# Transposes inside attention visits, a later last value product and sums behind the squares, in an attention and feed-forward kernel on one core

## The chip, the core and the metric

The kernel runs on one core of a Trainium2 chip. Five engines work beside each other, each through its own instructions in order: TensorE (PE in the profile, with its weight loads as PEld), VectorE (DVE), ScalarE (ACT), GpSimd (POOL) and SyncE (SP, which here only issues transfers). Transfers are issued from the queues of SP, POOL and ACT. The metric is the device time of one execution in microseconds (us), as the median of several.

## What is computed

Eight batches of 448 rows go through a squared-ReLU attention with 12 heads of 64, and the result through layer normalisation and a two-layer feed-forward block with a residual:

```python
scores = scale * np.matmul(q, k.transpose(0, 1, 3, 2))      # 8 x 12 x 448 x 448
attn = np.maximum(scores, 0.0) ** 2 / S
x = np.matmul(attn, v)                                      # heads side by side: 8 x 448 x 768
mu = np.mean(x, axis=-1, keepdims=True)
var = np.mean((x - mu) ** 2, axis=-1, keepdims=True)
xn = (x - mu) / np.sqrt(var + 1e-06) * g_ln
ch = np.maximum(xn @ w_ch1, 0.0) @ w_ch2                    # 768 -> 3072 -> 768
return x + ch
```

Inputs and output are float32; the products run in bfloat16.

## The kernel before

**Groups, batches, pairs.** The 12 heads of a batch are handled in three groups of four (`G` = 3), so there are 24 groups, numbered n = 3 b + m. Two batches make a pair; the feed-forward runs by pairs (four of them). A head's 448 rows are seven slices of 64 (`J` = 7).

**Attention of one group.** `scores` (L392) fills a PSUM tile with the products of one slice of keys (or two, in the first two batches) with the queries, on TensorE split into 64x64 tiles; ScalarE applies ReLU and moves it to SBUF (L411). The square is left to VectorE later: a tile waits in the list `later` (batches 0 and 1) or `fresh` (the others) until `squares_now` (L383) or `square_fresh` (L377) puts the multiplication into VectorE's order, at L389 or L380. Some squares run on ScalarE at once (L413). `values` (L421) multiplies by v (28 products, `av_ps`), and VectorE scales the result into `xT` (L438). Before a group's scores, queries and keys must be turned. For batches 0 and 1 TensorE does it: `piece` (L269) issues 14 transposes of 128x64 into one PSUM tile and a copy moves it out (L281); `transposes` (L286) calls it for q and for k. The later batches use transposing transfers from SP.

**PSUM.** Scores, value products and batch 1's transposes share three tiles (`ps_sc`); the feed-forward's results have two banks of their own (`ps_mm`). A tile that is asked for again waits until its last reader is done.

**Batch 1.** `attention_block(1, BLK[1][0])` makes a list of units for its first four slices: groups 3, 4 and 5, two score units each, one unit of transposes ahead of each group, a last value product and a centring. `interleave` (L13) sets them between the 26 units of batch 0's first feed-forward layer (`ffn1`, L718, six products into one `ps_mm` bank; `ffn1_head` takes three such at once). After the first ScalarE or VectorE work of a visit, `ffn1` lets VectorE move out the result of the one unit that follows a visit (`since`, L737), and ScalarE the next ones; right after it, it puts the waiting squares into VectorE's order.

**The three long stages.** For the pairs 0, 1 and 2 the second feed-forward layer of the pair runs beside the attention of the next two batches. `spread` (L28) takes the layer's parts (three products each) one by one and puts in a unit of attention when its share of work is due. A unit of attention is a bundle of three score slices, in some of them with the value product of the group before. After every other part `spread` puts one waiting square into VectorE's order, and before a bundle all of them. Between bundles come units of cost 0, the hooks: "even" after the first batch's values and "odd" when only the last group's values are missing. They make sums for the next layer-one stage, among them x[6] at L994, x[5] at L989 and, in the third stage, transfers on SP. When the units are used up or the parts end, the last value product comes, then "start" with the sums L905 and L906, then the parts that were held back (`few`), then the layer-one stage (`run`, L1017), which makes a 2x2 block product from seven products of half size. Its first steps combine partial results on VectorE at L1026, L1028, L1042 and L1045, and in the first pair weight sums at L936.

**What sets the order.** Each engine takes its instructions in the order in which the program issues them, so the Python order above is each queue's order.

Of the kernel before, what the change touches and what calls it, by code (L numbers as in the profile page):

```python
# [27 lines left out]
def spread(main, cost, side, costs, pending):  # L28

    period = (cost * len(main) + sum(costs)) / sum(c > 0 for c in costs)
    at, due, done, n, ago = 0, period - costs[0], 0, 0, 0
    for unit in main:
        unit()
        at += cost
        ago += 1
        if ago % 2:
            pending(1)
        if n < len(side) and at >= (due if costs[n] else done + 3 * cost):  # L40
            if costs[n]:
                pending()
            side[n]()
            if costs[n]:
                at += costs[n]
                due += period
                done = at
                ago = 0
            n += 1
    for unit in side[n:]:  # L50
        pending()
        unit()
    pending()
# [3 lines left out]
def kernel(  # L57
# [32 lines left out]
    J = S // HP  # L90
# [84 lines left out]
    def load(n, names):  # L175
        if n >= len(groups):
            return
        b, m = groups[n]
        for name in names:
            if b == 1 and name != "v":  # L180
                o = (2 * m + "qk".index(name)) * 2 * S
                t = hold[:, o:o + 2 * S].rearrange("p (r s) -> p r s", r=2)
            elif name == "q":
                t = qbuf[m][:, D:D + 2 * S].rearrange("p (r s) -> p r s", r=2)
            else:
                t = slot(name, n)
            nc.gpsimd.dma_start(t, srcs[name][b][:, m:NP:G, :])  # L187
            qkv[name, b, m] = t
# [72 lines left out]
    def idle(n):  # L261

        for _ in range(n):
            nc.tensor.matmul(idle_ps[:, 0, :P], ones, ones, start=True, stop=True)
# [4 lines left out]
    def piece(sb, b, m, n, lo, hi, bank=True):  # L269

        if b == 0 and bank:
            ps = ps_mm.tile([P, 1024], bf16, tag="mm", name="tr_ps")
        else:
            ps = ps_sc.tile([P, 2, 1024], bf16, tag="sc", name="tr_ps")[:, 0]
        src, i = qkv[n, b, m], "qk".index(n)
        for j in range(lo, hi):
            for pr in range(2):
                nc.tensor.transpose(  # L278
                    ps[pr * HP:(pr + 1) * HP, j * P:(j + 1) * P],
                    src[:, pr, j * D:(j + 1) * D], identity)  # L280
        return lambda copy, lo=lo, hi=hi: copy(  # L281
            sb[:, i * J + lo:i * J + hi, :], ps[:, lo * P:hi * P].rearrange("p (j c) -> p j c", c=P))

    held = []

    def transposes(b, m):  # L286


        if b == 0:
            o = 12 * 1024 + m * 2 * J * P  # L290
            sb = early[:, o:o + 2 * J * P].rearrange("p (i c) -> p i c", c=P)
        elif m:
            o = (m - 1) * 2 * J * P
            sb = hold[:, o:o + 2 * J * P].rearrange("p (i c) -> p i c", c=P)
        else:
            sb = slot("qT", G)
        dve, act = nc.vector.tensor_copy, nc.scalar.copy
        if (b, m) == (0, 0):
            nc.vector.tensor_copy(identity_g, identity[:K1, :K1])

            cast(dve, "q", 0, FEW)
            cast(act, "k", 0, FEW)
            cast(act, "k", FEW, J)
            idle(30)
            piece(sb, b, m, "q", 0, FEW)(dve)
            idle(2)
            piece(sb, b, m, "k", 0, FEW)(dve)
            idle(5)
        else:
            q_of = piece(sb, b, m, "q", 0, J)  # L310
            if (b, m) == (0, 1):

                q_of(act, 0, FEW)
            else:
                q_of(dve)
            k_of = piece(sb, b, m, "k", 0, J)
            if (b, m) == (0, 2):
                k_of(dve, 0, 3)
                held.append(lambda: k_of(act, 3, J))
            elif (b, m) == (0, 1):  # L320
                k_of(dve, 0, 3)
                k_of(dve, 3, J)
                q_of(dve, FEW, J)
            else:
                k_of(dve)
        if b:
            squares_now()
        st[b, m] = {
            "q": lambda i, r: sb[:, 0:J],
            "k": lambda i: sb[:, J + i],  # L330
            "where": lambda pr, j: (j, pr),
            "attn": [], "sb": sb}
# [209 lines left out]
    def transposed(n):  # L542

        if groups[n][0] < by_dma:
            transposes(*groups[n])
            return


        if by_dma * G < n < LATE:
            load(n + 2, "kq")  # L550
        keys_dma(n)
        queries_dma(n)
        if n == LATE + 1:
            put_off.append((n + 2, "kq"))
        elif n >= LATE:
            load(n + 2, "kq")

    def attention_block(b, blk):


        lo, hi, first = b * G, b * G + G, blk[0] == 0
        units = [lambda: transposed(lo)] if first else []

        def unit(n, part):
            squares_now()
            for i in range(4 * part, min(4 * part + 4, J), 2):
                scores(n, tuple(range(i, min(i + 2, J))), blk)
            if b == 1 and not first and part and n == hi - 1:
                transposed(hi)
            if part and n > lo:  # L570
                values(n - 1, blk)
                if not first:
                    load(n + 3, "v")
        for n in range(lo, hi):
            units.append(lambda n=n: unit(n, 0))
            if first and n + 1 < hi:
                units.append(lambda n=n: transposed(n + 1))
            units.append(lambda n=n: unit(n, 1))

        def last():  # L580
            values(hi - 1, blk)
            if b == 1 and not first:
                load(hi + 3, "v")
        units.append(last)
        units.append(lambda: centre(b, blk))
        return units
# [813 lines left out]
    for pair in range(pairs - 1):  # L1400
        last = pair == pairs - 2
        following = {}

        def hook(name):
            if not following:
                following.update(ffn1_pair(
                    pair + 1, keep=pair == 0, given=pair > 0, late=last,
                    between=(between_one, between_two, between_three)[pair]))
                if pair:
                    tokens_room(pair + 1)  # L1410
            following[name]()
            if (pair, name) in soon:
                tokens_part(pair + 1, *soon[pair, name])
        if last:
            mm = [ps_mm.tile([P, 512], fp32, tag="mm", name="o_ps") for _ in range(2)]
            zs = [x_room.rearrange("p b c s -> p (b c s)")[:, 3 * KH * P:3 * KH * P + 2 * DH].bitcast(fp32),
                  room0[:, 9:].rearrange("p c n -> p (c n)").bitcast(fp32)]
            h_sum_tiles()
            head, units, _ = strassen_units(pair, mm, lambda t: mm[::-1] if t % 2 else mm)
        else:  # L1420
            units = ffn2_units(pair)
            head, units = (units[:PARTS // 2], units[PARTS // 2:]) if pair else ([], units)
        if pair:
            for unit in head:
                unit()
            stage["close"]()
            if pair == 1:
                odd_h_out(pair, nc.sync, (8, KH), (8 + KH, K2))
            narrow.close()
            ps_sc = open_wide()  # L1430
        else:
            units = fold_beside(units)
        if pair == 1:
            w2_sum_tiles()
            units = beside_of(units, dict(zip((20, 36, 50), w2_sum_units("t6"))))
        beside, costs, left = attention(
            [2 * pair + 2, 2 * pair + 3], {G - 1: lambda: hook("even"), 2 * G - 2: lambda: hook("odd")})
        few = 3 * PARTS // 4
        spread(units[:-few], K2 // PARTS * DH, beside, costs, square_fresh)
        for f in left:  # L1440
            f()
        wide.close()
        hook("start")
        ps_m = open_narrow()
        for unit in units[-few:]:
            unit()
        store_now()
        stage = following
        if pair == 0:
            tokens(pair + 1)  # L1450
        stage["run"]()
        if pair == 0:
            statistics(pair + 1, 0)
            roots(pair + 1, 0, 1)
# [44 lines left out]
```

## Time and profile before

| | |
|---|---|
| median of 3 runs | 513.37 us (512.39 to 513.43) |
| time of the profiled execution | 512.57 us |
| its span in the trace | 510.6 us |
| PE busy | 503.1 us (99%), granted clock 1.0 |
| PEld / DVE / ACT / POOL busy | 297.9 / 388.2 / 315.3 / 130.0 us |
| stretch of batch 1's first part beside layer one | about 38 to 64 us |
| long stages (layer two beside attention) | 99 to 167, 214 to 274 and 321 to 390 us |
| layer-one stages between them | 167 to 214, 274 to 321 and 390 to 437 us |

The profile's page gives the busy time of each engine, the span in slices and the chain of work that ended last, followed back from the last instruction. The views of the trace used here are that chain in order of time (start, length, what) and the timeline (start, length, engine, line, operation, tiles; in brackets how long the engine had been idle and who ended it). TensorE's ends are modelled, so its starts and the chain's lengths are the better measure.

### The profile page before, as it was taken

The numbers are of one execution on the slowest core, as the hardware profiler recorded it, in microseconds if no ns is written. First come the engines' busy times: TensorE is split into PE (matmuls) and PEld (weight loads), VectorE is DVE, ScalarE is ACT, GpSimd is POOL, SyncE is SP. The second block draws the span as 40 slices with busy tenths as digits, with TensorE's granted clock in tenths as the row PEclk, the third lists the DMA queues.
The fourth block names the chain that finished last, engine by engine and source line by source line (L and its number), as shares of the span: only waits on it lengthen the run. The fifth ranks groups of instructions, "written<-read, shape, count | busy, mean of one in ns | idle before, by whom it ended". The sixth has DMA issues, their size and how long they took to land.

```text
span 510.6 us, 11501 instructions
## 1 busy us (share of the span) xinstructions
PE 503.1 (99%) x4545; PEld 297.9 (58%) x4545; DVE 388.2 (76%) x747; ACT 315.3 (62%) x519; POOL 130.0 (25%) x180
## 2 busy tenths in 40 slices
PE   8999999999999999999999999999999999999996
PEld 6677778955555555555555555555555555566663
DVE  4875755697998988768878888578869688677663
ACT  5966776578887566667883666489884677300000
POOL 8335102011412486002111995011000231000000
PEclk9999999999999999999999999999999999999999
DMA  9999999999999975739993878349936943622222
GB/s 198 206 206 206 211 206 143 135 195 177 203 203 223 219 228 152 191 87 163 269 170 75 177 167 140 61 78 179 194 69 164 224 131 94 230 64 63 63 62 62
DMA packets 136743, 80.25 MB, mean 157 GB/s; under 512 B 92418, under 2 KB 132610, under 8 KB 136690
## 3 DMA queue, kind: packets, MB, share of 16 engines
q1 hardware_dynamic: 106402, 46.59, 43.9%
q0 software_dynamic: 28272, 29.92, 36.7%
q10 hardware_dynamic: 2016, 3.02, 2.4%
q8 instruction: 35, 0.57, 0.5%
q14 instruction: 18, 0.15, 0.1%
HBM read 66.65 MB, written 19.86 MB: 169 GB/s over the span
## 4 chain that ended last, share of the span: by engine, by line
PE 92%; DMA 5%; POOL 1%; ACT 1%; DVE 1%; issue 1%; DVEq 0%; ACTq 0%; POOLq 0%
PE m_ps L960 28%; PE o_ps L789 17%; PE m_ps L1175 11%; PE o_ps L1175 11%; PE h_ps L728 7%; PE sc_ps L400 7%; PE av_ps L432 6%; DMA w<-in_moe_w_ch_dram 3%; PE h_ps L773 2%; DMA v_sb<-in_v_dram 2%; PE o_ps L1136 2%; PE h_ps L755 1%; ACT attn_sb L411 1%; PE tr_ps L278 1%; PE sum_ps L465 0%
## 5 line engine op out<-in xcount | busy, mean ns | idle before, releaser
L411 ACT ACTIVATE attn_sb<-sc_ps 128x896 bf16<-128x896 f32 (+4 forms) x150 | 126.2, 902 | 27.1 <-PE sc_ps L400 20.8
L964 ACT ACTIVATE hT_sb<-m_ps 128x448 bf16<-128x448 f32 x144 | 78.2, 543 | 51.8 <-PE m_ps L960 49.1
L789 PE MATMUL o_ps<-w,hT_sb 128*128 128x384 bf16 x528 | 92.2, 327 | 0.0
L789 PEld LDWEIGHTS <-hT_sb 128*128 128x128 bf16 x528 | 49.0, 98 | 39.8 <-issue 10.1
L380 DVE TENSOR_TENSOR attn_sb<-attn_sb 128x896 bf16<-128x896 bf16 x93 | 55.6, 617 | 8.0 <-ACT attn_sb L411 8.0
L728 PE MATMUL h_ps<-x_room,w 128*128 128x192 bf16 (+2 forms) x384 | 44.0, 263 | 0.2 <-DMA w<-in_moe_w_ch_dram 0.2
L438 DVE TENSOR_SCALAR xT_sb<-av_ps 128x896 bf16<-128x896 f32 (+2 forms) x30 | 27.1, 903 | 22.3 <-PE av_ps L432 22.2
L1175 PEld LDWEIGHTS <-hT_sb 128*128 128x128 bf16 x312 | 30.0, 98 | 21.6 <-issue 2.1
L1175 PEld LDWEIGHTS <-x_room 128*128 128x128 bf16 x288 | 27.5, 98 | 20.2 <-issue 2.5
L728 PEld LDWEIGHTS <-w 128*128 128x128 bf16 x384 | 33.8, 97 | 7.2 <-issue 1.8
L960 PEld LDWEIGHTS <-w 128*128 128x128 bf16 x246 | 24.0, 97 | 22.7
L1042 DVE TENSOR_TENSOR m_ps<-x_room,m_ps 128x448 f32<-128x448 f32 x36 | 22.6, 628 | 18.4 <-ACT hT_sb L964 18.2
L413 ACT ACTIVATE attn_sb<-attn_sb 128x896 bf16<-128x896 bf16 x33 | 31.4, 950 | 1.0
L960 PEld LDWEIGHTS <-w_sum 128*128 128x128 bf16 x210 | 20.5, 98 | 19.3 <-DVE w_sum L936 0.4
L705 DVE BATCH_NORM_STATS2 stats<-xtok_sb 128x6 f32<-128x384 bf16 x56 | 28.3, 547 | 3.1 <-DMA xtok_sb<-xT_sb 3.1
L187 POOL DMA_DIRECT2D k_sb<-in_k_dram x15 | 10.7, 711 | 78.2 <-DMA kT_sb<-k_sb 51.3
L187 POOL DMA_DIRECT2D v_sb<-in_v_dram x20 | 14.2, 715 | 61.1 <-PE sc_ps L400 52.4
L519 DVE SCALAR_TENSOR_TENSOR w<-w,g_sb,x_room 128x512 bf16<-128x512 bf16 x36 | 27.3, 787 | 3.0 <-ACT x_room L515 3.0
L960 PE MATMUL m_ps<-x_sum,w 128*128 128x448 bf16 x120 | 29.1, 352 | 0.0
L1024 ACT COPY x_room<-m_ps 128x448 f32<-128x448 f32 x36 | 19.1, 532 | 15.4 <-PE m_ps L960 14.4
L400 PE MATMUL sc_ps<-qT_sb,kT_sb 64*64 64x448 bf16 x392 | 27.9, 358 | 0.0
L432 PE MATMUL av_ps<-attn_sb,v_sb 64*64 64x448 bf16 (+2 forms) x532 | 26.9, 331 | 0.4 <-DVE attn_sb L380 0.4
(202 smaller groups left out, 895.5 us busy)
## 6 DMA issues: line engine op xcount, KB each, us to landing
out_dram<-o_room SPq DMA_DIRECT2D x108, 96.0 KB, 2.4
w<-in_moe_w_ch_dram POOLq DMA_DIRECT2D x12, 384.0 KB, 14.3
w<-in_moe_w_ch_dram POOLq DMA_DIRECT2D x4, 1152.0 KB, 20.1
q_sb<-in_q_dram POOLq DMA_DIRECT2D x20, 224.0 KB, 5.7
v_sb<-in_v_dram POOLq DMA_DIRECT2D x20, 224.0 KB, 5.8
k_sb<-in_k_dram POOLq DMA_DIRECT2D x15, 224.0 KB, 5.3
kept<-room SPq DMA_DIRECT2D x4, 480.0 KB, 3.2
kept<-w_sum SPq DMA_DIRECT2D x16, 96.0 KB, 2.4
```

The costliest lines, as they stand in the source:

```text
L380: nc.vector.tensor_mul(a, a, a)
L400: nc.tensor.matmul(ps[cols, r, o * w:(o + 1) * w], g["k"](i)[rows, cols], g["q"](i, r)[rows, blk[0]:sum(blk), cols], start=True, stop=True)
L411: nc.scalar.activation(a, ps[:, :, :len(slots) * w], ACTF.Relu)
L413: nc.scalar.activation(a, a, ACTF.Square)
L432: nc.tensor.matmul(ps[cols, hh, :w], v_sb[rows, pr, j * D:(j + 1) * D], g["attn"][i][rows, r, :], start=(j == 0), stop=(j == J - 1))
L519: nc.vector.scalar_tensor_tensor(w, w, g_sb[:, c:c + 1], fold["means"][i % 2].rearrange("p (h n) -> p h n", h=2), op0=ALU.mult, op1=ALU.add)
L705: nc.vector.bn_stats(stats[:, n], xtok[pair][:, n * G:(n + 1) * G, t, :])
L728: nc.tensor.matmul(ps[:, :w + more], w1[:, c, ni * P:(ni + 1) * P], xc[b][:, c, s.start:s.stop + more], start=(c == 0), stop=(c == K1 - 1))
L789: nc.tensor.matmul(ps[:, :DH], hT[pair][:, ki, t * P:(t + 1) * P], w2[:, ki, cols], start=(o == 0), stop=(o == K2 - 1))
L960: nc.tensor.matmul(ps, *at, start=(first and c == 0), stop=(c == KQ - 1), skip_group_check=not first)
L964: nc.scalar.activation(hT[pair][:, n + KH * row, half * S:(half + 1) * S], ps, ACTF.Relu)
L1175: nc.tensor.matmul(ps, x[:, ki], y[ki] if isinstance(y, list) else y[:, ki], start=(first and ki == 0), stop=(ki == KH - 1), skip_group_ch ...
```

## The change

Three places change. In batch 1, the transposes of groups 4 and 5 are no longer units of their own: the queries are turned at the end of the first score unit of the group before, the keys at the end of the second one. `spread` no longer takes the last unit of attention inside its loop, and puts all waiting squares ahead of hooks too. And the parts held back behind the last value product (`few`) are four instead of six.

```diff
@@ spread
-        if n < len(side) and at >= (due if costs[n] else done + 3 * cost):
-            if costs[n]:
-                pending()
+        if n < len(side) - 1 and at >= (due if costs[n] else done + 3 * cost):
+            pending()
             side[n]()
@@ transposes
-    def transposes(b, m):
+    def transposes(b, m, name=None):
...
+        elif name:
+            piece(sb, b, m, name, 0, J)(dve)
+            if name == "q":
+                return
         else:
             q_of = piece(sb, b, m, "q", 0, J)
...
@@ attention_block, unit(n, part)
                 values(n - 1, blk)
                 if not first:
                     load(n + 3, "v")
+            if first and n + 1 < hi:
+                transposes(*groups[n + 1], "qk"[part])
         for n in range(lo, hi):
             units.append(lambda n=n: unit(n, 0))
-            if first and n + 1 < hi:
-                units.append(lambda n=n: transposed(n + 1))
             units.append(lambda n=n: unit(n, 1))
@@ the three long stages
-        few = 3 * PARTS // 4
+        few = PARTS // 2
         spread(units[:-few], K2 // PARTS * DH, beside, costs, square_fresh)
```

`transposes` ends, for batch 1 and whenever it did not return early, with `squares_now()`, which puts every waiting square into VectorE's order. `PARTS` is 8.

## Prediction

> **What bounds the kernel.** First the page's chain of work that ended last:
>
> ```profile
> PE 92%; DMA 5%; POOL 1%; ACT 1%; DVE 1%; issue 1%; DVEq 0%; ACTq 0%; POOLq 0%
> ```
>
> TensorE sets the end, at granted clock 1.0 in every slice. Its product count is not changed, so only time in which TensorE waits or changes its tiles can move. I then read the chain in order of time round each place of the change; it shows where TensorE waits for others:
>
> ```profile
> 58.07 0.45 PE sc_ps L400 x12
> 58.52 0.90 PE av_ps L432 x28
> 59.43 1.43 PE h_ps L728 x12
> 60.85 1.12 PE av_ps L432 x28
> ...
> 162.59 1.48 PE av_ps L432 x28
> 164.07 3.03 PE o_ps L789 x18
> ...
> 269.28 0.77 DVE x_room L994
> 270.05 0.55 DVE attn_sb L380
> 270.60 0.04 issue
> 270.64 0.57 PE av_ps L432 x7
> 271.21 3.03 PE o_ps L789 x18
> ...
> 385.80 1.81 PE av_ps L432 x28
> ```
>
> The three value products of 448 columns are the last ones of the long stages. Behind scores such a product takes 1.32 in the chain; standing alone it pays a change of tiles, 0.12 (below), so 1.44. The first (1.48) waits 0.04, the second (2.25 from 268.96 to 271.21, of which some 0.07 before 269.03 is the part ahead of it) 0.74, the third 0.37. In the second, a square (L380) stands behind the hook's sum L994 in VectorE's order: that is what "sums behind squares" turns round.
>
> **1. Batch 1's transposes.** Two units of 28 transposes disappear, and 14 transposes join each of four score units.
>
> *Tile changes, 0.* The nearest rows are at the program's start, where transposes follow scores directly:
>
> ```profile
> 6.18 0.36 PE L400 MATMUL sc_ps<-early 64*64 64x192 bf16 x8
> 6.47 0.41 PE L278 MATMUL tr_ps<-identity,k_sb 128*64 128x128 bf16 x8
> ```
>
> Score visits of 256 columns take 0.56 for 16 and 0.45 for 12, so 0.0275 each and 0.12 fixed; eight of 192 columns would need 0.165 and take 0.29 from start to start: 0.125 for going from 64x64 tiles to 128x64. Layer two shows the same on its side (3.52 for 21 products, 2.54 for 15: 0.163 each and 0.09 fixed). Two visits removed save four changes, four visits gain one each: 0. If the inner change cost nothing, -0.5; if it cost 0.15, +0.1. I take 0.
> The Trainium skill (TensorEngine Tiling (Array Packing), Key Properties) says that a change of tiling mode drains the engine. Counted by visits the change would bring 0.5, counted by that rule nothing; the 0.125 above agrees with the rule.
>
> *Last value product, -0.24.* `interleave` places 11 units behind main units 3, 5, 7, ... 21, 23, and 9 behind 3, 6, 8, 11, 13, 16, 18, 21, 23 (side units times i over 23, as three of the 26 are free). Group 5's last product now has three layer-one units ahead of it, not two. At 60.85 it took 1.12 against 0.76 behind scores plus 0.12: 0.24 waiting for the squares (60.60 to 61.62). 0.7 more cover removes it. Between -0.24 and 0.
>
> *A bank of layer one, +0.75.* After the second unit of group 3 the keys' copy and both squares now go into VectorE's order at once, ahead of the next layer-one result. Before, the result goes first:
>
> ```profile
> 47.63 1.49 PE L728 MATMUL h_ps<-x_room,w 128*128 128x258 bf16 x12
> 48.50 0.16 DVE L735 COPY fold_sums<-h_ps 128x2 f32<-128x2 f32 x1 [1.45 <-PE h_ps L728]
> 48.58 0.41 DVE L737 TENSOR_SCALAR hT_sb<-h_ps 128x256 bf16<-128x256 f32 x1
> 48.91 1.01 DVE L389 TENSOR_TENSOR attn_sb<-attn_sb 128x1024 bf16<-128x1024 bf16 x2
> ```
>
> From the visit's start: scores 0.45, transposes 0.50 (28 take 0.90 with a change, and 14 ahead of 14 others 0.41, from 8.80 to 9.21), then VectorE: copy from 1.04 for 0.58 (half of 1.15), squares 1.01, result 0.49: 3.1, and 0.06 to signal. TensorE has done two more units by 0.95 + 1.43 = 2.38 and the third (now three stand together) needs the bank: 0.75 of waiting. Queued behind it on TensorE are the next visit and everything after. Bounds 0 (VectorE early) and 0.9. The other three visits do not pay: with queries `squares_now` is not called, and after `values` ScalarE takes the results.
>
> *A score tile, +0.10.* In group 4's second visit the keys' transposes are the fourth user of three tiles and need its first scores' ReLU, done at 1.43 (0.46 to begin, 0.97), while TensorE arrives at 1.33. Between 0 and 0.2.
>
> Sum of part 1: 0 - 0.24 + 0.75 + 0.10 = +0.61. The transposes' inputs are there: POOL's last such load is issued at 35.8 and lands 10.8 later, its reader comes at 51.
>
> **2. Ends of the long stages.** Adding up `spread`'s costs, the last bundle, the odd hook and the last value product stand after parts 85, 88, 90 (first stage), 66, 69, 70 and 81, 84, 86; in the new program after 87, 90, 92; 68, 71, 72; 83, 86, 88. So the distance from the last scores to the last value product stays; the new bound in the loop changes nothing, as the last unit was outside it already. What moves is the distance to the layer-one stage: two parts or six products, 0.98 us at 0.163 each.
>
> *Gain.* First stage: the third square is ScalarE's, the wait was 0.04. Second: three squares on VectorE; the third now ends about 3.63 after the bundle's start (ReLU to 2.90, square 0.62), before the product's 22nd step (2.75 + 1.11), and L994 after it still ends with the product: -0.74. Third: there the square of the second slice stood behind a result and a difference (L1193, L1238) that waited for TensorE's part 84; now part 84 comes right after the bundle, and the squares end at 3.6, before they are needed: -0.37. Sum -1.15; bounds -1.15 and 0.
>
> *Loss.* After the last value product VectorE has a fixed list: scaling, sums, results, then L1026. The two parts less are taken from its cover. Second stage:
>
> ```profile
> 271.25 1.09 DVE L438 TENSOR_SCALAR xT_sb<-av_ps 128x896 bf16<-128x896 f32 x1 [0.66 <-PE av_ps L432]
> 274.62 0.62 DVE L800 SCALAR_TENSOR_TENSOR o_room<-o_ps,rstd_sb,xtok_sb 128x384 f32<-128x384 f32 x1
> 275.48 0.62 DVE L1026 TENSOR_TENSOR x_room<-x_room,m_ps 128x448 f32<-128x448 f32 x1 [0.25 <-ACT x_room L1024]
> 277.58 0.62 DVE L1042 TENSOR_TENSOR m_ps<-x_room,m_ps 128x448 f32<-128x448 f32 x1
> ```
>
> With E the product's end (271.21), VectorE can begin L1026 at E + 3.95 (0.54 after L800). The stage starts at E + 3.03 before, E + 2.05 after, and L1026's input is there 1.24 later: E + 3.29. Late by 0.66. The slack is read at 278.62, where TensorE takes the bank that L1042 leaves at 278.20: 0.36 with the signal. TensorE waits 0.30.
> First stage: L1026 possible at E + 3.71, wanted at E + 3.30: 0.41 late. Here there is no slack:
>
> ```profile
> 171.06 0.30 PEld L960 LDWEIGHTS <-w_sum 128*128 128x128 bf16 x3 [0.42 <-DVE w_sum L936]
> ```
>
> TensorE already waits for L936 (about 0.16), so +0.41.
> Third stage: the hook's two sums (0.85 each) and one result now stand ahead of the scaling, which begins at E + 0.93. The sums for the stage's third product are ready at E + 2.97, just as it comes; one result later L1026 begins at E + 4.27, against E + 3.33 in the old distance: 0.94 late, slack 0.33 (394.69 against 395.02): +0.61.
> Each of these lies between 0 (VectorE squeezes the list) and its full lateness plus slack lost: 0.57, 0.66, 0.97. Sum +1.32.
>
> *Moved with them, 0.* The odd hook of the third stage issues transfers on SP, 0.98 nearer to their use: weights issued by 385.9 with 4.2 to land, first read at 393.1; if that cover of 3 us were gone, the lateness would go to TensorE whole. SP's token transposes (386.46, 7.64 long) and stores behind them keep their order. The last groups' loads on POOL and transposes on SP go two parts later, for groups that are used a layer-one stage (46 us) later. GpSimd's first weight sum in the first stage starts 0.98 nearer: ready at E + 4.0, read at E + 4.7. The squares ahead of the "even" hook delay sums not read for tens of us.
>
> Part 2: -1.15 + 1.32 = +0.17. **Sum:** 0.61 + 0.17 = +0.78. The profiled execution took 512.57 (span 510.6 and 1.97 round it), 0.8 under the median; added to it, 513.35. Against the median of 513.37: 514.15, written 514.2.
>
> **Rivals.** *A, the gains come and the costs don't* (the bank is freed in time, the stages' heads absorb the late sums): -0.24 - 1.15 = -1.39, or -1.9 with free inner tile changes: 512.0. For it: the waits of 0.74 and 0.37 are on the chain. Against: TensorE waits for L936 even now.
> *B, VectorE becomes the bound at the heads of the layer-one stages:* after L1045 it goes on to the next L1026 without idling (278.11, then 278.65), so lateness above 0.36 there is not made up before the next block and TensorE pays it whole: 0.57 + 0.66 + 0.97 = 2.2 instead of 1.32, and 0.9 for the bank: 513.37 + 0.78 + 0.88 + 0.15 = 515.2. Against: VectorE idles 1.11 before the second L1042.
> *C, it doesn't do what it says:* "later" leaves the distance to the scores as it was, so if the first and third stages neither gain nor lose, the second pays its whole lateness (-0.74 + 0.66) and the inner change of tiles is free (part 1 at +0.1), all cancels: 513.4. Against: it needs three coincidences.
>
> **Chances.** Forecast 0.50, A 0.20, B 0.22, C 0.08. The forecast's own range is 513.6 to 515.0. About 0.2%, 1.03 us, is what a measurement of this kernel can tell from no change: 512.34 to 514.40. The forecast lies inside for 0.27 and above for 0.23; so faster 0.20, same 0.35, slower 0.45. Range: from A's 512.0 to B's 515.2 and a little beyond for the bounds of the bank and of the third stage: 511.9 to 515.7.
>
> **What would show it.** Right: transposes behind scores 0.12 apart; a wait of TensorE for VectorE's L737 near 48.5; the last value products all at 1.4 to 1.5; TensorE waiting at L960 for L936 and L1042 early in the three layer-one stages. Wrong: no such wait at 48.5 (then about 0.75 less), or layer-one stages as long as before (46.77, 46.67 and about 46.5 in the chain).

## The result, and the profile after

The changed kernel takes 514.15 us (median of 10 runs) against 512.66 for the kernel before on the same chip: the ratio is 1.0028, interval 1.0019 to 1.0038, so 1.0 to 1.9 us or 0.2 to 0.4% slower. The profiled span went from 510.6 to 512.1 us. The forecast of 514.2 stands beside 514.15, but it was made on a median of 513.37 for the kernel before; against the median of these runs the step is 1.49, where the sum said 0.78. That the two times meet to 0.05 us is luck: a base that is 0.71 too high made up for a sum that is 0.71 too small.

The traces say where it went. Line numbers of the changed kernel are two higher in the functions behind the change (L960 is L962, L1026 is L1028). The table cuts each profiled execution at six marks on TensorE: batch 1's first transposes to its centring, the first long stage's first layer-two product to the second stage's, and so on to the last layer-two stage. Each of the three long columns thus holds one long stage's end and the layer-one stage behind it.

| us in the trace | batch 1's part | first | second | third |
|---|---|---|---|---|
| before | 22.38 | 114.01 | 107.03 | 116.27 |
| changed | 23.34 | 114.42 | 106.73 | 116.63 |
| difference | +0.96 | +0.41 | -0.30 | +0.36 |

Together +1.43; between the marks nothing else moved (36.46 and 36.45 us from the centring to the first long stage). These lines of the chain of work in order of time (start, length, what) are the changed kernel's, round group 3's second visit and group 4's, and at the first stage's end. The two lines of the second block are from the kernel before, for comparison: 28 transposes between layer-one products, and what follows them.

```profile
46.73 0.51 PE tr_ps L277 x14
47.24 1.44 PE h_ps L730 x12
...
49.20 0.82 PE h_ps L730 x6
50.02 0.56 PE sc_ps L402 x16
50.58 0.51 PE tr_ps L277 x14
...
53.01 0.94 ACT attn_sb L413
53.95 0.04 issue
53.99 0.58 PE tr_ps L277 x14
54.57 2.12 PE h_ps L730 x18
...
62.16 0.89 PE av_ps L434 x28
...
164.60 1.55 PE av_ps L434 x28
```

```profile
44.92 0.90 PE tr_ps L278 x28
45.82 1.43 PE h_ps L728 x12
```

TensorE stops between 48.68 and 49.20, the chain leaves it for ScalarE ahead of 53.99, fourteen transposes take 0.51 behind scores, and group 5's last value product takes 0.89, not 1.12. Where three layer-one units stand together, as from 54.57 on, the third one waits too, if only a little. These lines are of the timeline there, the last one of the view from 56.01 on, so that it holds the third unit alone:

```profile
55.43 0.39 ACT L741 ACTIVATE hT_sb<-h_ps 128x256 bf16<-128x256 f32 x1
55.87 0.82 PE L730 MATMUL h_ps<-x_room,w 128*128 128x258 bf16 x6
```

ScalarE has emptied the first unit's bank at 55.82, and 0.05 later the third unit starts. Its first product starts 0.15 after the product ahead of it, where the others start 0.11 apart.

The heads of the three layer-one stages, from the changed kernel's timeline of TensorE (start, length, engine, line, operation, tiles; in brackets the idle time and its releaser):

```profile
169.73 0.73 PE L962 MATMUL m_ps<-x_room,w 128*128 128x448 bf16 x3
170.49 0.73 PE L962 MATMUL m_ps<-x_sum,w 128*128 128x448 bf16 x3
171.06 1.30 PE L962 MATMUL m_ps<-xT_sb,w_sum 128*128 128x448 bf16 x6
172.53 0.74 PE L962 MATMUL m_ps<-x_sum,w_sum 128*128 128x448 bf16 x3 [0.17 <-DVE w_sum L938]
...
271.40 1.52 PE L434 MATMUL av_ps<-attn_sb,v_sb 64*64 64x448 bf16 x28
272.85 2.12 PE L791 MATMUL o_ps<-w,hT_sb 128*128 128x384 bf16 x12
...
276.51 0.73 PE L962 MATMUL m_ps<-x_room,w 128*128 128x448 bf16 x3
277.53 0.73 PE L962 MATMUL m_ps<-x_sum,w 128*128 128x448 bf16 x3 [0.29 <-DVE x_room L1028]
...
387.88 1.52 PE L434 MATMUL av_ps<-attn_sb,v_sb 64*64 64x448 bf16 x28
389.33 2.12 PE L1177 MATMUL o_ps<-spare,hT_sb 128*128 128x384 bf16 x12
391.43 1.29 PE L962 MATMUL m_ps<-xT_sb,room 128*128 128x448 bf16 x6
...
393.13 0.73 PE L962 MATMUL m_ps<-qT_sb,w 128*128 128x448 bf16 x3
394.28 0.73 PE L962 MATMUL m_ps<-x_sum,w 128*128 128x448 bf16 x3 [0.42 <-DVE x_room L1028]
```

A group of three starts 0.57 after the one ahead of it where nothing waits. So the step from 276.51 to 277.53 holds 0.45 of waiting, and that from 393.13 to 394.28 0.58. In the first stage the step to 170.49 holds 0.19 at the same place, and the six from 171.06 take 1.47 instead of 1.14, so 0.33 of waiting for L938 (0.14 in the kernel before). In the kernel before, the product that now waits at 277.53 started without a wait:

```profile
275.78 0.73 PE L960 MATMUL m_ps<-x_room,w 128*128 128x448 bf16 x3
276.35 0.73 PE L960 MATMUL m_ps<-x_sum,w 128*128 128x448 bf16 x3
```

The last value products of the second and third stage now take 1.45 from start to the next start, without a wait.

### The profile page after: what moved, and what is told of

It is laid out like the page before. It is cut to its first block, busy times and chain, and to the rows that moved or that the text cites. A ratio compares the mean times of both kernels' runs of the same rounds, so it can differ in the third digit from the quotient of the medians.

```text
span 512.1 us, 11500 instructions
## 1 busy us (share of the span) xinstructions
PE 503.2 (98%) x4545; PEld 298.4 (58%) x4545; DVE 388.3 (76%) x747; ACT 316.0 (62%) x519; POOL 130.0 (25%) x180
## 4 chain that ended last, share of the span: by engine, by line
PE 92%; DVE 4%; ACT 2%; issue 1%; DVEq 0%
PE m_ps L962 26%; PE o_ps L791 16%; PE m_ps L1177 11%; PE o_ps L1177 10%; PE h_ps L730 8%; PE sc_ps L402 7%; PE av_ps L434 6%; PE h_ps L775 2%; ACT early L413 2%; PE h_ps L757 2%; PE o_ps L1138 2%; PE tr_ps L277 1%; PE idle_ps L263 1%; DVE xT_sb L440 1%; DVE x_sum L907 1%
## 5 line engine op out<-in xcount | busy, mean ns | idle before, releaser
L382 DVE TENSOR_TENSOR attn_sb<-attn_sb 128x896 bf16<-128x896 bf16 x93 | 57.4, 636 | 7.1 <-ACT attn_sb L413 6.6
L440 DVE TENSOR_SCALAR xT_sb<-av_ps 128x896 bf16<-128x896 f32 (+2 forms) x30 | 27.1, 904 | 22.7 <-PE av_ps L434 22.5
L962 PEld LDWEIGHTS <-w 128*128 128x128 bf16 x246 | 24.0, 97 | 24.0 <-issue 1.5
L962 PEld LDWEIGHTS <-w_sum 128*128 128x128 bf16 x210 | 20.5, 98 | 19.5 <-DVE w_sum L938 0.6
L962 PE MATMUL m_ps<-x_sum,w 128*128 128x448 bf16 x120 | 29.0, 352 | 0.7 <-DVE x_room L1028 0.7
L521 DVE SCALAR_TENSOR_TENSOR w<-w,g_sb,x_room 128x512 bf16<-128x512 bf16 x36 | 25.8, 744 | 3.0 <-ACT x_room L517 3.0
L1177 PE MATMUL m_ps<-w,x_room 128*128 128x384 bf16 x156 | 27.2, 326 | 0.0
L1026 ACT COPY x_room<-m_ps 128x448 f32<-128x448 f32 x36 | 19.2, 532 | 11.5 <-PE m_ps L962 10.6
```

The lines of the kernel that those rows point to most:

```text
L382: nc.vector.tensor_mul(a, a, a)
L440: nc.vector.tensor_scalar_mul(x, ps[:, :, :w], score_scale)
L962: nc.tensor.matmul(ps, *at, start=(first and c == 0), stop=(c == KQ - 1), skip_group_check=not first)
L1177: nc.tensor.matmul(ps, x[:, ki], y[ki] if isinstance(y, list) else y[:, ki], start=(first and ki == 0), stop=(ki == KH - 1), skip_group_ch ...
```

## The experiments

All are measured against the kernel before, run on the same chip beside them (median 512.97 beside the first four rows, 512.84 beside the next three, 513.22 beside the last two). Each kernel has its own line numbers, so one statement's line differs by a few between the fences. Single runs of one kernel differ by up to 2 us and more, so the intervals are wide, and the traces are cut at the same marks as above. A star marks a stretch in which that profiled run waited for a late transfer (see the last section). The runs of the hook's squares and of "and weight sum first" also lost 0.75 and 0.54 between the table's columns, ahead of the first long stage.

| us in the trace | batch 1's part | first | second | third | median | ratio to before, interval |
|---|---|---|---|---|---|---|
| transposes alone | 23.34 | 114.64* | 107.03 | 116.27 | 513.89 | 1.0015, 1.0004 to 1.0027 |
| transposes, late squares | 22.74 | 114.01 | 107.03 | 116.27 | 513.01 | 0.9998, 0.9987 to 1.0009 |
| ends alone | 22.37 | 114.41 | 106.71 | 116.64 | 513.40 | 1.0005, 0.9992 to 1.0018 |
| four parts alone | 22.37 | 114.42 | 107.17 | 116.64 | 513.81 | 1.0015, 0.9996 to 1.0035 |
| hook's squares alone | 22.37 | 115.85* | 106.30 | 116.27 | 511.90 | 0.9979, 0.9962 to 0.9995 |
| last results out | 23.34 | 114.26 | 106.38 | 116.10 | 513.14 | 1.0009, 0.9998 to 1.0020 |
| a square each part | 22.37 | 113.99 | 106.30 | 115.92 | 512.36 | 0.9980, 0.9965 to 0.9994 |
| and weight sum first | 22.37 | 113.93 | 106.29 | 115.92 | 512.07 | 0.9976, 0.9952 to 1.0000 |
| weight sum first alone | 22.38 | 115.42* | 107.01 | 116.27 | 513.14 | 0.9991, 0.9966 to 1.0016 |

**Transposes alone** takes the changed kernel and sets the ends back:

```diff
-        if n < len(side) - 1 and at >= (due if costs[n] else done + 3 * cost):
-            pending()
+        if n < len(side) and at >= (due if costs[n] else done + 3 * cost):
+            if costs[n]:
+                pending()
             side[n]()
...
-        few = PARTS // 2
+        few = 3 * PARTS // 4
```

> Only batch 1's transposes are put into the attention visits; the long stages' ends stay as before. From the changed kernel's trace (the centring of batch 1 comes 0.97 later behind the same start): 0.9 to 1.0 us slower than before, with a wait of TensorE for VectorE's L739 of some 0.5 near 48.7 and one for a score tile of 0.25 near 53.9. If the two parts of the change need each other (the rival: the loss at the start is caught up later, when layer one's weights are ready anyway), within 0.2 us of before.

The trace gives +0.96 in batch 1's part and nothing at the second and third end, the times +0.92 (median against 512.97). Nothing is caught up later, so the rival falls. The wait near 48.7 is there, in this kernel's timeline:

```profile
47.06 0.62 DVE L281 COPY xtok_sb<-tr_ps 128x896 bf16<-128x896 bf16 x1
47.60 1.02 DVE L392 TENSOR_TENSOR attn_sb<-attn_sb 128x1024 bf16<-128x1024 bf16 x2
48.53 0.39 ACT L742 ACTIVATE hT_sb<-h_ps 128x256 bf16<-128x256 f32 x1
48.60 0.42 DVE L740 TENSOR_SCALAR hT_sb<-h_ps 128x256 bf16<-128x256 f32 x1
48.98 0.82 PE L731 MATMUL h_ps<-x_room,w 128*128 128x258 bf16 x6 [0.54 <-ACT hT_sb L742]
```

Copy and squares go first and VectorE gets to the layer-one result at 48.53 (its small copy, L738), though TensorE had issued that unit's products by 47.7. The releaser is ScalarE's L742, which empties the other bank; VectorE's own result ends 0.1 later still. So neither bank was free, and the third unit waited 0.54.

**Transposes, late squares** is the run of the transposes alone without `squares_now` in the transposes inside visits:

```diff
-        if b:
+        if b and not name:
             squares_now()
```

> As the transposes alone, but the transposes in visits do not put the waiting squares into VectorE's order; the next layer-one unit does it behind its own result. If the wait for a bank comes from the squares standing ahead of that result: 0.4 to 0.55 faster than the transposes alone, so 0.4 to 0.5 slower than before. If three layer-one units standing together or the tile changes make the loss (the rival): as slow as the transposes alone.

Batch 1's part falls by 0.60 against the transposes alone, the times by 0.88. That is a little more than the 0.4 to 0.55 expected. In its timeline the result goes ahead of the squares, and eighteen layer-one products stand in one row:

```profile
47.00 2.25 PE L731 MATMUL h_ps<-x_room,w 128*128 128x258 bf16 x18
...
47.94 0.41 DVE L740 TENSOR_SCALAR hT_sb<-h_ps 128x256 bf16<-128x256 f32 x1
48.27 1.01 DVE L392 TENSOR_TENSOR attn_sb<-attn_sb 128x1024 bf16<-128x1024 bf16 x2
```

VectorE's result ends at 48.35, the third unit starts at 48.41, 0.20 after the product ahead of it; the pace is 0.11. So of the 0.70 that TensorE loses there in the transposes alone, the squares' place makes 0.6, and three units standing together 0.09. What is left, +0.36, is read from the starts of single products in its trace: 0.24 ahead of the third units of four rows (0.08, 0.09, 0.04, 0.04), 0.32 at the score tile (0.25 of waiting, and a first transpose that comes later after it), -0.23 at group 5's last product. That leaves 0.03 for changes of tiles. The times do not confirm the +0.36 as they stand (the medians differ by 0.04, with an interval of -0.7 to +0.5); the lowest times differ by 0.41 (512.75 against 512.34).

**Ends alone** puts the change of `spread` and of `few` on the kernel before.

```diff
-        if n < len(side) and at >= (due if costs[n] else done + 3 * cost):
-            if costs[n]:
-                pending()
+        if n < len(side) - 1 and at >= (due if costs[n] else done + 3 * cost):
+            pending()
             side[n]()
...
-        few = 3 * PARTS // 4
+        few = PARTS // 2
```

> Only the long stages' ends are changed: all squares ahead of hooks, four parts held back. By the two traces +0.4 in the first stage's end, -0.3 in the second's, +0.37 in the third's: 0.4 to 0.5 slower than before. If the ends and the transposes are not independent (the rival): within 0.2 of before or 1 us slower.

+0.40, -0.32, +0.37: the changed kernel's three differences, without the transposes. In the traces the two halves of the change add up. By its times alone (+0.43) this run could not be told from before; the trace decides.

**Four parts alone** keeps `spread` and changes `few`:

```diff
-        few = 3 * PARTS // 4
+        few = PARTS // 2
```

> Only the number of parts held back goes from six to four; hooks stay ahead of the last square. If the lateness of VectorE's list behind the last value product is what costs: +0.4, about 0 and +0.35 at the three ends, so 0.6 to 0.9 slower than before, and in the second stage the last value product waits some 0.3 again behind L994. If holding back fewer parts were what brings the second stage's gain (the rival): 0.4 to 0.5 slower, no wait there.

+0.41, +0.14, +0.37 in the trace, +0.84 in the medians. In the second stage L994 is ahead of the last square again, as VectorE's timeline shows:

```profile
269.88 0.62 DVE L380 TENSOR_TENSOR attn_sb<-attn_sb 128x896 bf16<-128x896 bf16 x1 [0.18 <-ACT attn_sb L411]
270.42 0.85 DVE L994 TENSOR_TENSOR x_room<-xT_sb 128x1344 bf16<-128x1344 bf16 x1
271.19 0.62 DVE L380 TENSOR_TENSOR attn_sb<-attn_sb 128x896 bf16<-128x896 bf16 x1
```

The last value product takes 1.93 there instead of 1.45. So fewer parts bring loss at all three ends. In the second, a result (L800) moved out of the squares' way and the wait fell from 0.74 to 0.48; the rest stays with the hook's sum, so the gain of the change there is mostly its order.

**Hook's squares alone** keeps six parts:

```diff
-            if costs[n]:
-                pending()
+            pending()
```

> Only the squares go ahead of hooks; six parts are held back as before. If the order of L994 and the last square is what made TensorE wait in the second stage: its last value product falls from 2.2 to 1.45, the stage behind it starts as before, 0.6 to 0.8 us faster than before; the first and third stage do not move, since all their VectorE squares stand ahead of the odd hook anyway. If the square is late for another reason (the rival: ScalarE's ReLU): within 0.2 of before.

-0.73 in the second column, 0 in the third; the first holds the late transfer. The chain of its second stage's end:

```profile
269.37 2.06 PE o_ps L788 x12
271.42 1.45 PE av_ps L431 x28
272.87 3.03 PE o_ps L788 x18
275.90 2.27 PE m_ps L959 x12
```

The value product has lost its wait and the layer-one stage follows without one. The order of the sum and the square is shown as the cause, and taken alone it makes the kernel faster by its times (0.2%), though the profiled run itself took 514.22, with the late transfer in it.

**Last results out** asks whether VectorE's list sets the heads. This kernel leaves out the last result of each long stage, so VectorE has one instruction less there and a part of the output is not written:

```diff
-        if part < parts - 1:
+        if part < parts - 1 or omit[0]:
             return
...
         def result(ps, row, half):
+            if omit[0]:
+                return
...
+        omit[0] = True
         for unit in units[-few:]:
             unit()
+        omit[0] = False
```

> The changed kernel without the last result of each of the three long stages: one half-width result and its two transfers each are left out, so VectorE's list behind the last value product is one instruction of 0.54 shorter. If that list sets the start of the layer-one stages: 0.19 + 0.33, 0.45 and 0.45 to 0.55 less waiting, so 1.2 to 1.5 us faster than the changed kernel and about as fast as before. If a PSUM bank handed over from the scores or a transfer sets it (the rival): within 0.2 us of the changed kernel.

Against the changed kernel -0.16, -0.35 and -0.53, 1.04 together, and 1.0 in the medians (514.15 and 513.14). The second head runs through, at 0.57 a step:

```profile
275.57 0.73 PE L963 MATMUL m_ps<-x_sum,room 128*128 128x448 bf16 x3
276.13 0.73 PE L963 MATMUL m_ps<-x_room,w 128*128 128x448 bf16 x3
276.70 0.73 PE L963 MATMUL m_ps<-x_sum,w 128*128 128x448 bf16 x3
```

The rival of a bank or a transfer falls, except for 0.14 at the third head (391.43 in the changed kernel, when VectorE's scaling, L440, lets go of the scores' last tile); another 0.06 of waiting for VectorE's list is left there. In the first stage less came than expected, mostly for a reason in the last section.

**A square each part** changes the kernel before only in how often a square is put in:

```diff
-        if ago % 2:
-            pending(1)
+        pending(1)
```

> The kernel before with one waiting square put into VectorE's order after each part, not after every other one. All three squares of a bundle then stand ahead of the odd hook, and in the third stage the second square stands ahead of part 84's result. If VectorE's order is what the last value products wait for: -0.74 in the second stage, -0.37 in the third, 1.0 to 1.2 us faster than before. If ScalarE's ReLU or TensorE's own order makes the third stage's wait (the rival): -0.74 alone. If earlier squares hold up results behind them in the stages' middle: less, down to nothing.

-0.02, -0.73 and -0.35 in the trace, whose span is 509.4. In the third stage the second square now stands ahead of part 84's result, as VectorE's timeline shows:

```profile
383.88 0.63 DVE L379 TENSOR_TENSOR attn_sb<-attn_sb 128x896 bf16<-128x896 bf16 x1 [0.18 <-ACT attn_sb L410]
384.42 0.61 DVE L1192 SCALAR_TENSOR_TENSOR o_room<-o_ps,rstd_sb,xtok_sb 128x384 f32<-128x384 f32 x1
```

The value product behind it takes 1.45. So both waits were a matter of VectorE's order, and no part had to move. By its ratio, 0.9980 (0.9965 to 0.9994), this kernel is faster than both.

**The weight sum first** moves one line in `run` for the first layer-one stage, once on top of the last kernel and once alone:

```diff
                 if n == 0:
+                    if not given:
+                        sums_late(1)
                     x_sum(7, lo[:, KQ:], hi[:, KQ:], nc.vector.tensor_sub)
...
                     if n:
                         sums_early(n + 2)
-                    sums_late(n + 1)
+                        sums_late(n + 1)
```

> A square after each part, and in the first layer-one stage VectorE makes the second block's weight sum (L936) ahead of x[7]'s sums, which are needed 0.6 later. If VectorE's order is all that TensorE waits for there: the 0.16 it waits for L936 before goes too, so 1.1 + 0.15 = 1.2 to 1.3 us faster than before. If x[7]'s sums then come too late (the rival), 1.0 to 1.1 faster, with a wait at the block's seventh product.

> The kernel before with that swap alone. By the trace's wait of 0.16 for L936: 0.1 to 0.16 us faster, less than the runs can tell by their times, so read from the start of the second long stage in the trace (213.71 before). If the wait only moves to x[7]'s sums (the rival): no shift.

On top, 0.06 of the 0.16 came. TensorE now steps from 171.38 to 172.05 ahead of its seventh product, 0.67 and not 0.57, so 0.10 of the wait moved there:

```profile
171.08 0.38 DVE L905 TENSOR_TENSOR x_sum<-xT_sb 128x448 bf16<-128x448 bf16 x1
171.38 0.62 DVE L1043 TENSOR_TENSOR m_ps<-x_room,m_ps 128x448 f32<-128x448 f32 x1
172.05 0.73 PE L959 MATMUL m_ps<-x_sum,room 128*128 128x448 bf16 x3
```

The rival has the place right, but not the reason. The sums of x[7] are done at 171.46; what ends at 172.00, 0.05 ahead of the product, is L1043 (L1042 before), which leaves the bank into which this product adds. VectorE's list is as long as it was, and L1043 comes no earlier. The run alone says nothing: a store landed late just there and held VectorE for 0.88.

## Why the prediction came out, step by step

The direction held, and so did the two main mechanisms, squares ahead of a bank's reader and a VectorE list that comes too late. The time was met by luck: the sum of 0.78 was half of the 1.43 in the traces. Its terms:

- *Tile changes*, put at 0: measured +0.03 to +0.05, so this held. 28 transposes take 0.90 and 14 take 0.51, so 14 more cost 0.39, and 0.12 is left for the inner change (0.125 forecast). The two visits that go also save the fixed part of two layer-one stretches: products start 0.11 apart, and 12 take 1.43, so 0.1 for each stretch, near the 0.09 read from layer two. Together 2.04 against 1.80 + 0.20.
- *Group 5's last product*, -0.24: measured -0.23.
- *A bank of layer one*, +0.75: measured 0.70 (0.53 of waiting by the profile, and the stretch that it breaks). The squares' place is shown as the cause for 0.6 of it; the bank was the other one. A step failed beside it: the other three visits were to pay nothing, but the third unit behind a visit waits for its bank there as well, 0.08, 0.04 and 0.04 in the trace, 0.16 together.
- *A score tile*, +0.10: measured 0.32. This term was too small. The ReLU was done 1.41 into the visit, as forecast (1.43), but TensorE came at 1.21, not 1.33: a value product behind scores pays no tile change (0.76). That makes 0.25 of waiting, and 0.07 more pass until the transposes are at their pace.
- *Gain at the ends*, -0.04, -0.74, -0.37: the last two came whole; the first product takes 1.55 instead of 1.48, so nothing came there.
- *Loss at the ends*, 0.41, 0.30, 0.61: with the gains taken out of the table it is 0.4, 0.44 and 0.73. The lateness was right, 0.66 in the second stage, but here the second step failed: the slack of 0.36 was read at the wrong reader. TensorE first needs L1028's read (L1026 before) of the bank into which the second product of the block goes, and there the slack was 0.2 (the read ended at 276.10, the product started at 276.35 before, with 0.05 for the signal). In the first stage 0.19 of the loss sits at the same reader and the rest at L938, where all of it was forecast. In the third stage 0.14 at the tile handed over comes on top, which the forecast did not price.
- *Rival A* had the gains without the costs: the costs are shown, though the gains alone make a faster kernel. *Rival B* had VectorE late without slack; the truth lies between it and the forecast. *C* falls.
- That the new bound in `spread` changes nothing was argued from the costs and not tried by itself. The 0.04 to 0.08 ahead of the third units are read from one trace each and not tested by a run.

## What to carry to other kernels

On an engine that is not the bottleneck, an instruction costs what it holds up behind it rather than its own length: here squares ahead of a bank's reader cost 0.6 us, and a sum ahead of a square 0.73. And when a sum of small terms lands on the measured time, compare it term by term, against runs of the same session: here half of the cost was missing, and the total hid it. Before cover is taken from a list of work, find the first reader that the list holds up, not the one that looks tightest. When a change bundles an edit that gains with one that loses, run each alone: the gain here needed one line (`pending(1)` after each part).

## What was not expected

Two adds side by side slowed each other. In the run without the last results VectorE's sum L909 took 0.61 us instead of 0.38, while GpSimd's weight sum took 0.87 instead of 0.42:

```profile
170.51 0.87 POOL L927 TENSOR_TENSOR w_sum<-w 128x128 bf16<-128x128 bf16 x1
171.01 0.61 DVE L909 TENSOR_TENSOR x_sum<-xT_sb 128x448 bf16<-128x448 bf16 x1
```

It gave back 0.23 of what was saved there. The Trainium skill (SBUF — State Buffer, SBUF: two separate sides) says that a VectorE operation with two SBUF inputs and a GpSimd operation that reads SBUF block each other for a whole instruction; the two times agree with it. The run with the weight sum first alone has such a pair too: its L936 took 1.12 on VectorE, 0.55 in the kernel before, and the GpSimd sum beside it 0.75 instead of 0.42.

Stores are one source of spread in the traces. The output leaves from three buffers; a store lands after 2.4 us in the median, but one took 7.9 in the profiled run of the hook's squares, and VectorE, which needed the buffer, waited 2.4 and TensorE behind it. The same happened for 0.88 in the run with the weight sum first, and a weight transfer (`kept<-w_sum`) was late in the run with the transposes alone. These are the starred stretches. The 0.75 and 0.54 ahead of the first long stage, near 98.5 us, are something else: the trace names ScalarE (L775) for the one and no engine for the other, and why TensorE stops stays open.
